# A recurrent attention block with a gated feed-forward block on one core: fewer, wider idle products, level one in one piece, and a shift behind a masked copy

## The chip, the core and the metric

The kernel runs on one core of a Trainium2 chip. The time is what the device takes for one execution, in microseconds (us). The engines have short names: PE (TensorE, the matrix array; its weight loads are shown apart as PEld), DVE (VectorE), ACT (ScalarE), POOL (GpSimd) and SP (SyncE, which here only issues transfers). Each engine runs its own instructions in order and waits for others through semaphores.

## What is computed

The first block is a linear attention with a decaying state, for 4 batches, 8 heads, 768 steps and head size 48. The second multiplies the result (3072 tokens of 384) by a weight to 2048, applies a gate, and multiplies back to 384. All is in float32.

```python
for t in range(S):
    cur = np.einsum('bhd,bhe->bhde', u[None] * kt, vt)
    y[:, :, t] = np.einsum('bhd,bhde->bhe', rt, state + cur)
    state = wt[:, :, :, None] * state + np.einsum('bhd,bhe->bhde', kt, vt)
x = y.transpose(0, 2, 1, 3).reshape(B * S, H * D)
h = x @ w_in
sp = np.maximum(h, 0.0) + np.log1p(np.exp(-np.abs(h)))
out = (h * erf(sp)) @ w_out
```

## The kernel before

The 768 steps are cut into 12 stages of 64. Stage s does the attention of its 64 steps for all batches and heads, while pieces of the feed-forward block of earlier stages run between its parts: six products against `w_in` are one piece of `hidden` (three contraction blocks for each of two blocks of features), and `project` multiplies by `w_out`.

**Levels.** Inside a stage the attention is built by doubling. At level L, `level_products` multiplies the keys of the left halves of blocks of 2^L steps by the queries of the right halves into a bank of PSUM called `pp` (there are two, used in turn). `take_level` then copies the masked part into `own` (a predicated copy on DVE), and `scale` multiplies keys and queries in place by the decays of their half blocks (on DVE, by totals that POOL makes), which the products of the next level need. At level one the products use `rk1`, where u is already multiplied in, and one DVE product with the mask `first` starts `own`. Six levels make a stage's 64 steps. Then `from_own` multiplies `own` by v into `y`, `fence` copies a few elements of y into `seen` so that others can wait for it, and `through_state` adds the carried state's part and lays y out as `xT`, which the feed-forward block reads. In stage 0 the last step of this is `hop`: three products with the 0/1 matrix `apart` shift rows, and DVE adds the result to xT.

**Stage 0** is `attend_first`. It has no older pieces to run beside it. So it has idle products, whose results nobody reads: `stay_warm(24)` at the beginning of the program, `stay_warm(4)` behind each half of level one's products, and `keep_busy(..., 4)` behind the products of levels two to five. Both multiply 128 columns at a time, `stay_warm` with the identity on both sides, `keep_busy` with a state that is still zero. The products go in two halves (batches of two), and so do the scalings of stage 0. The stages overlap at their borders: of the 32 products of stage 1's level one, twelve are issued behind level six of stage 0, twelve behind `through_state`, and the last eight in stage 1 itself, behind the first piece of `hidden`.

**Conversion of the weights.** The weights come as float64, two words an element, and are turned into float32 in 16 chunks (8 of `w_in`, 8 of `w_out`), each in stages with one letter: "l" the load (SP), "b" ACT scales the high word into a base in PSUM, "r" ACT scales the low word, "h" a shift on DVE, "o" an add on POOL, "j" the shift and the add. `send` runs the next chunk of each letter, `stages["h"](3)` a given chunk. The loads have three buffers, and a small copy on POOL or ACT into a buffer (`behind`) holds a load back until some other work is done.

**Order.** The kernel is written under a manual schedule: every engine runs its instructions in the order in which the Python code emits them. `place(n)` is called once a level by `attend`; it emits conversions (`convert_at`), feed-forward pieces (`beside`) and activations (`advance`). SP's queue has the loads in the same order of emission.

Lines for the prediction: L970 `stay_warm`, L976 `keep_busy`, L657 `level_products`, L880 and L1023 the product of level one with `first`, L667 the masked copy, L327 and L334 `scale`, L919 ACT's copies of level six in stage 0, L698 `fence`, L1131 the products of `hidden`, L1140 their copy out of PSUM, L258 and L260 "b", L275 "h", L288 "o", L768 the products for the state, L1162 `project`.

Of the kernel before, what the change touches and what calls it, by code (L numbers as in the profile page):

```python
# [11 lines left out]
FP32 = mybir.dt.float32  # L12
# [5 lines left out]
P = 128  # L18
# [4 lines left out]
NJ = 2  # L23
FG = 8
FT = 2

# [33 lines left out]
def kernel(  # L62
# [789 lines left out]
    def attend_first(xT):  # L852
# [10 lines left out]
        pp = products([P, NE, JP, HC])  # L863
        for half in halves:
            level_products(pp, by_pair(made), 1, half)
            stay_warm(4)
        nc.scalar.copy(first[:], mask_sb[:, 0, :])
        totals(1, part=slice(0, batch))
        for j in range(NJ):
# [15 lines left out]
        for level in range(2, LOG):  # L885
            pp = turns.pop("pp", None) or products([P, NE, JP, HC])
            for j, half in enumerate(halves):
                level_products(pp, first_pair, level, half)
                scale(0, level, batch=j)
            turns["pp"] = products([P, NE, JP, HC])  # L890
            keep_busy(turns["pp"], 4)
            take_level(own, pp, level)
            wait_for(1 << level - 1)
            if level == 2:
                totals(2, part=slice(batch // 2, batch))
            else:
                totals(*behind[level])
            if level == 2:
                stages["b"](0, 0)
                stages["b"](0, 1)  # L900
                stages["r"](0)
                for _ in prepare(1):
                    pass
                nc.sync.dma_start(out=vt[:], in_=v[0])
                stages["l"](1, own[:, 0, 2:3])
                nc.sync.dma_start(out=ws[1][:], in_=rkw[1][:, 2])
# [29 lines left out]
        stages["h"](1)  # L936
        totals(1)
        through_state(0, xT)
        level_products(turns["pp"], second, 1, range(3, 6))
        turns.pop("hop")()  # L940
        stages["r"](1)
        stages["o"](1)
# [23 lines left out]
    def stay_warm(times):  # L966

        for _ in range(times):
            ps = ps_m.tile([P, P], FP32, name="m")
            nc.tensor.matmul(ps[:], lhsT=ident[:], rhs=ident[:], start=True, stop=True)  # L970

    def keep_busy(pp, times):

        zeros = states[0][:].rearrange("p h n d -> p (h n d)")
        for _ in range(times):
            nc.tensor.matmul(  # L976
                pp[:].rearrange("p e n t -> p (e n t)")[:, :P], lhsT=ident[:],
                rhs=zeros[:, :P], start=True, stop=True, skip_group_check=True,
            )

    def attend(s, xT, early, place, behind):

        in_t, vt, made, _, _ = parts_of(s)
        K = in_t[:, 1]
        RK = by_pair(in_t)


        following = prepare(s + 1) if s + 1 < n_steps else iter(())
        own = made if s >= DIRECT else att.tile([P, NH, HC], FP32, name="own")

        if s == DIRECT:
            next(following)
        for level in range(near_log(s) + 1 if s == DIRECT else 1, LOG + 1):
            rk = by_pair(made) if level == 1 else RK
            pp = turns.pop("pp", None) or products([P, NE, JP, HC])
            if s == level == 1:
                send("br")
            elif s != 2 or level != 2:
                level_products(pp, rk, level)
            if level == LOG and s == DIRECT:  # L1000
                spread_blocks(s + 1, pp)
            if s == 1 and 2 < level:
                stages["h"](level + 1)
            scale(s, level)
            if s == 1 and level in turns["pending"]:
                turns["pending"].pop(level)()
            if s == 1 and level == 2:
                stages["h"](level + 1)
            if s == 1 and level > 1:
                nc.gpsimd.tensor_copy(out=block_sb[:, 0:1], in_=K[:, 0, 0:1])  # L1010
                for i in {2: (2, 3)}.get(level, (level + 1,)):
                    stages["o"](i)
            if s == 2 and level > 1:
                hold(K[:, 0, 0:1])
                send("o")
            if s != 1:
                early(level - 1)
            got = pp[:].rearrange("p e n t -> p (e n) t")
            if s == level == 1:
                place(0)  # L1020
                level_products(pp, rk, 1, range(6, JP))
            if level == 1:
                nc.vector.tensor_mul(  # L1023
                    own[:], got, first[:, None, :].to_broadcast([P, NH, HC])
                )
                if s == 1:
                    stages["h"](2)
            else:
                take_level(own, pp, level)
            if (s, level) == (DIRECT - 1, 4):  # L1030
                hold(K[:, 0, 0:1])
                fade_state(s)
            if level > 1 and (s, level) != (1, 4):
                next(following, None)
            if s == 2 and level == 1:

                def ahead():
                    turns["pp"] = products([P, NE, JP, HC])
                    level_products(turns["pp"], RK, 2)

                turns["ahead"] = ahead
            if (s, level) != (1, 1):
                place(level - 1)
            if (s, level) == (1, 4):
                next(following, None)
            if s == 1 and level in (3, 4):
                nc.sync.dma_start(out=loaded[2][0][:, level - 3], in_=rkw[2][:, level - 3])

        from_own(s, own, 1)
        ps = products([P, JP, P])  # L1050
        for n in range(JP):
            nc.tensor.transpose(ps[:, n, :], K[:, n, :], ident[:])  # L1052
        kT = att.tile([P, NH, D], FP32, name="kT", bufs=1)
        nc.scalar.copy(
            kT[:].rearrange("p (e n) d -> p e n d", e=NE),
            ps[:].rearrange("p n (e d) -> p e n d", e=NE)[..., :D],
        )
        if s != DIRECT - 1:
            fade_state(s)
        next(following, None)  # L1060
        place(LOG)
        if s == DIRECT - 1:
            for _ in range(3):
                mixing.send(nc.vector)

        ps = products([P, NC, JP, HC])
        state_part(s, kT, ps)
        from_own(s, own, 0)
        next_state(s, ps)
        for _ in following:  # L1070
            pass
        place(LOG + 1)
        through_state(s, xT)
        behind()
# [442 lines left out]
    with tc.manual_schedule(  # L1517
        engines={getattr(mybir.EngineType, x) for x in ("PE", "DVE", "Activation", "Pool", "SP")}
    ):
        stay_warm(24)  # L1520
        for t in states:
            nc.gpsimd.memset(t[:], 0.0)
        nc.gpsimd.memset(over_blocks[:], 1.0)
# [9 lines left out]
        for s in range(n_steps):  # L1533
# [7 lines left out]
            def place(n):  # L1541
# [7 lines left out]
                if s in ALONE:  # L1549
                    if s == 2 and not n:  # L1550

                        next(hids[0])
                        turns.pop("ahead")()
                    if (s, n) != (1, 0):
                        convert_at(n)
                    if (s, n) == (1, LOG - 1):
                        load_w(3)
# [4 lines left out]
                        nc.sync.dma_start(out=u_row[:], in_=u_rows)  # L1562
                    if s == 2 and not n:
                        beside(s, next(places))
                        advance(STAGES[s][n])
                        return
                    advance(STAGES[s][n])
# [131 lines left out]
```

## Time and profile before

| | |
|---|---|
| median of 3 runs | 587.57 us (587.5 to 589.57) |
| profiled execution, its own time | 589.73 us |
| its span, first to last instruction | 587.9 us |
| busy: PE, DVE, ACT, POOL | 577.2, 427.4, 355.0, 242.2 us |
| mean granted clock of TensorE | 0.991 |
| PE busy from 0 to 32.5 / 32.5 to 71 / 71 to 587.9 | 28.65 / 35.20 / 513.38 us |

The page of the profile gives the busy time of each engine, and the span in 40 equal slices with the granted clock of TensorE in tenths. The trace can also be asked for windows (busy time of each engine in a stretch, with the granted clock, the share of the DMA engines and the rate), for a timeline (start, duration, engine, line, operation, written tile <- read tiles, shape, count, and in brackets the idle time before it and what ended it) and for waits. A matrix product in float32 appears as two records on PE and two weight loads on PEld. Matmuls are pipelined and their ends are modelled, so the start of the next group tells more than the end of the last. A releaser named "issue" means that the profile shows nothing that the engine waited for.

### The profile page before, as it was taken

How to read it: one execution, taken by the hardware profiler on the slowest of the kernel's cores; microseconds unless marked ns; L12 is line 12 of the kernel's file. 1: busy time of each engine (PE TensorE's matmuls, PEld its weight loads, DVE VectorE, ACT ScalarE, POOL GpSimd, SP SyncE). 2: the span in 40 equal slices, each digit the busy share in tenths (PEclk: the TensorE clock that was granted, in tenths of full speed). 3: DMA queues.
4: the chain of work that ended last, by engine and by line, in shares of the span. 5: the costliest groups of instructions: out<-in, count | busy, mean ns of one | idle time of the engine just before them, and what ended most of it. 6: DMA issues, size and time to landing. Idle time of an engine off the chain costs nothing.

```text
span 587.9 us, 16633 instructions
## 1 busy us (share of the span) xinstructions
PE 577.2 (98%) x7302; PEld 501.3 (85%) x7302; DVE 427.4 (73%) x451; ACT 355.0 (60%) x478; POOL 242.2 (41%) x263
## 2 busy tenths in 40 slices
PE   8989899999999999999999999999999999999997
PEld 8877788668768857899899899899899899988997
DVE  5677495799796699699599599599599537256530
ACT  3376698817544398675775765765865861387700
POOL 2187266520884776277077077067065000000000
PEclk9699999999999999999999999999999999999999
DMA  7388173532226226236236236235231101000111
GB/s 256 107 288 341 56 276 108 222 81 83 97 75 190 42 95 197 46 108 198 49 106 199 47 107 198 46 108 163 47 107 28 19 10 35 1 2 1 28 28 27
DMA packets 52057, 62.04 MB, mean 106 GB/s; under 512 B 33392, under 2 KB 38800, under 8 KB 50960
## 3 DMA queue, kind: packets, MB, share of 16 engines
q1 hardware_dynamic: 51360, 60.58, 33.8%
q8 instruction: 57, 0.93, 0.7%
q10 hardware_dynamic: 624, 0.39, 0.3%
q14 instruction: 16, 0.13, 0.1%
HBM read 51.60 MB, written 8.27 MB: 102 GB/s over the span
## 4 chain that ended last, share of the span: by engine, by line
PE 87%; ACTq 0%; ACT 0%; issue 0%; DVE 0%
PE m L1131 32%; PE m L1244 28%; PE m L1162 11%; PE pp L1332 4%; PE pp L657 4%; PE y L1332 2%; PE y L689 2%; PE y L712 2%; PE pp L768 1%; PE pp L1052 1%; PE pp L1244 0%; ACTq L756 0%; PE pp L781 0%; ACT y L260 0%; DVE o L1276 0%
## 5 line engine op out<-in xcount | busy, mean ns | idle before, releaser
L1131 PE MATMUL m<-xT,w_in_sb 128*128 128x256 f32 x960 | 214.2, 381 | 1.5 <-ACT y L260 1.5
L1131 PEld LDWEIGHTS m<-xT,w_in_sb 128*128 128x128 f32 x960 | 180.1, 190 | 26.5 <-ACT y L260 1.6
L334 DVE TENSOR_TENSOR in<-in,tot_sb 128x1024 f32<-128x1024 f32 (+1 forms) x55 | 77.7, 1412 | 20.7 <-PE pp L657 19.7
L1140 ACT COPY h<-m 128x512 f32<-128x512 f32 x80 | 46.4, 580 | 61.7 <-PE m L1131 61.7
L1162 PE MATMUL m<-w_out_sb,h 128*128 128x384 f32 x192 | 64.3, 491 | 0.0
L1162 PEld LDWEIGHTS m<-w_out_sb,h 128*128 128x128 f32 x192 | 35.7, 190 | 23.5
L1244 PE MATMUL m<-mixed,h 128*128 128x192 f32 x256 | 45.6, 331 | 0.0
L1244 PE MATMUL m<-w_out_sb,h 128*128 128x192 f32 x256 | 44.8, 329 | 0.0
L1244 PEld LDWEIGHTS m<-mixed,h 128*128 128x128 f32 x256 | 41.4, 190 | 0.9
L1091 ACT ACT_TABLE_LOAD x30 | 38.5, 1283 | 6.0 <-DVE h L1096 5.6
L1244 PEld LDWEIGHTS m<-w_out_sb,h 128*128 128x128 f32 x256 | 41.6, 190 | 0.3
L657 PEld LDWEIGHTS pp<-in 48*48 48x48 f32 (+4 forms) x2368 | 31.9, 125 | 11.4 <-issue 6.5
L1244 PE MATMUL m<-w_out_sb,room 128*128 128x192 f32 x240 | 41.5, 326 | 0.0
L464 POOL TENSOR_TENSOR words<-words,own 128x384 f32<-128x384 f32 x21 | 31.0, 1476 | 22.5 <-DVE words L495 12.8
L457 POOL TENSOR_TENSOR own<-rest 128x384 f32<-128x384 f32 x7 | 10.4, 1482 | 71.3 <-ACT o L1250 44.4
L505 POOL TENSOR_TENSOR words<-words 128x384 f32<-128x384 f32 x28 | 39.7, 1447 | 0.0
L1087 ACT ACT_TABLE_LOAD x30 | 38.5, 1283 | 1.8 <-issue 1.3
L1244 PEld LDWEIGHTS m<-w_out_sb,room 128*128 128x128 f32 x240 | 39.4, 190 | 0.0
L657 PE MATMUL pp<-in 48*48 48x32 f32 (+4 forms) x2368 | 35.9, 211 | 1.8 <-issue 1.8
L617 POOL COPY faded<-s 128x1 f32<-128x1 f32 x10 | 12.4, 1240 | 53.8 <-DVE s L623 53.8
L530 DVE TENSOR_REDUCE sums<-rk 128x16 f32<-128x768 f32 (+2 forms) x31 | 31.6, 1021 | 0.0
L505 POOL TENSOR_TENSOR rk<-words 128x384 f32<-128x384 f32 x28 | 31.4, 1154 | 0.0
(200 smaller groups left out, 998.9 us busy)
## 6 DMA issues: line engine op xcount, KB each, us to landing
in<-in_rkw SPq DMA_DIRECT2D x8, 1024.0 KB, 5.4
words<-in_moe_w_in SPq DMA_DIRECT2D x16, 384.0 KB, 6.5
words<-in_moe_w_out SPq DMA_DIRECT2D x16, 384.0 KB, 6.1
words<-in_rk_rows SPq DMA_DIRECT2D x8, 768.0 KB, 7.3
w<-in_rkw SPq DMA_DIRECT2D x11, 512.0 KB, 6.4
v<-in_v SPq DMA_DIRECT2D x12, 384.0 KB, 5.7
out<-o SPq DMA_DIRECT2D x45, 96.0 KB, 2.8
in<-in_rkw SPq DMA_DIRECT2D x7, 512.0 KB, 5.3
```

The lines of the kernel that those rows point to most:

```text
L334: nc.vector.tensor_mul(halves, halves, view(tots[level - 1], 0, [[1, n], [2, nb], [0, half]]))
L464: engine.tensor_mul(to, to, of[:, :, None, :].to_broadcast([P, NEAR // 2 // half, half, D]))
L505: engine.tensor_mul(to[:, i], r[:, half:], k[:, part * rows + i, None].to_broadcast([P, half, D]),)
L530: nc.vector.tensor_reduce(out=to, in_=of, axis=mybir.AxisListType.X, op=ALU.add)
L657: nc.tensor.matmul(to, lhsT=rk(1, n)[rows(e), s0 : s0 + m], rhs=right, start=True, stop=True,)
L1087: nc.scalar.activation(sp_room, chunks[0], AF.Softplus)
L1091: nc.scalar.activation(at, sp_room, AF.Erf)
L1131: nc.tensor.matmul(ps[:, ff, :], lhsT=w_in_sb[:, g * FG + f + ff, kk * P : (kk + 1) * P], rhs=xT[:, kk, :], start=kk == 0, stop=kk == KT - 1,)
L1140: nc.scalar.copy(h[:, f : f + FT, :], ps[:])
L1162: nc.tensor.matmul(ps[j][:], lhsT=gs[g][:, f, j * C : (j + 1) * C], rhs=w_out_sb[:, g * FG + f, :], start=g + f == 0, stop=g == NG - 1 and ...
L1244: nc.tensor.matmul(to, lhsT=a[:, f], rhs=b[:, f], start=start and f == 0, stop=f == FG - 1, skip_group_check=True,)
L1332: nc.tensor.matmul(to[:, e], lhsT=a[:, 2 * i + e], rhs=b, start=start and not k, stop=True, skip_group_check=True,)
```

## The change

- The 24 opening idle products become 36 small ones (64 x 64 x 64, in the two opposite quarters of the array in turn) and 5 wide ones of 256 columns. Behind each half of level one, 4 of 128 columns become 2 of 256. Behind levels two to five, 4 of 128 become one of 384.
- The last eight products of stage 1's level one are issued with the twelve before them, ahead of the hop's shift products and so ahead of the first piece of `hidden`. DVE's product L1023 keeps its place among DVE's instructions.
- In stage 1, level two, the shift and the add of chunk 3 are emitted behind the masked copy, not before it.
- In stage 2, the conversion at its first place is emitted behind the piece `beside`; ACT's copy of that piece so comes ahead of the conversion's two ACT operations.

By the order in which the built programs stand, SP and POOL run the same instructions in the same order as before. On DVE one shift changes places with one masked copy, and L1023 loses its wait for PE. On ACT one copy changes places with two activations. On PE the idle products differ, and 8 products (16 records) move up.

```diff
+FEW = 36
@@ attend_first
             level_products(pp, by_pair(made), 1, half)
-            stay_warm(4)
+            stay_warm(2)
@@
             turns["pp"] = products([P, NE, JP, HC])
-            keep_busy(turns["pp"], 4)
+            keep_busy(turns["pp"])
             take_level(own, pp, level)
@@
         through_state(0, xT)
-        level_products(turns["pp"], second, 1, range(3, 6))
+        level_products(turns["pp"], second, 1, range(3, JP))
         turns.pop("hop")()
@@
     def stay_warm(times):
 
         for _ in range(times):
-            ps = ps_m.tile([P, P], FP32, name="m")
-            nc.tensor.matmul(ps[:], lhsT=ident[:], rhs=ident[:], start=True, stop=True)
-
-    def keep_busy(pp, times):
+            ps = ps_m.tile([P, NC, P], FP32, name="m")
+            nc.tensor.matmul(
+                ps[:], lhsT=ident[:], rhs=ident[:, None, :].to_broadcast([P, NC, P]),
+                start=True, stop=True,
+            )
+
+    def keep_busy(pp):
 
         zeros = states[0][:].rearrange("p h n d -> p (h n d)")
-        for _ in range(times):
-            nc.tensor.matmul(
-                pp[:].rearrange("p e n t -> p (e n t)")[:, :P], lhsT=ident[:],
-                rhs=zeros[:, :P], start=True, stop=True, skip_group_check=True,
-            )
+        nc.tensor.matmul(
+            pp[:].rearrange("p e n t -> p (e n t)")[:, :DM], lhsT=ident[:],
+            rhs=zeros[:, :DM], start=True, stop=True, skip_group_check=True,
+        )
@@ attend
-            if s == 1 and level == 2:
-                stages["h"](level + 1)
             if s == 1 and level > 1:
                 nc.gpsimd.tensor_copy(out=block_sb[:, 0:1], in_=K[:, 0, 0:1])
-                for i in {2: (2, 3)}.get(level, (level + 1,)):
-                    stages["o"](i)
+                stages["o"](2 if level == 2 else level + 1)
@@
-            if s == level == 1:
-                place(0)
-                level_products(pp, rk, 1, range(6, JP))
             if level == 1:
                 nc.vector.tensor_mul(
                     own[:], got, first[:, None, :].to_broadcast([P, NH, HC])
@@
             else:
                 take_level(own, pp, level)
+                if s == 1 and level == 2:
+                    stages["h"](3)
+                    stages["o"](3)
@@
-            if (s, level) != (1, 1):
-                place(level - 1)
+            place(level - 1)
@@ the program's start
-        stay_warm(24)
+        few = ps_m.tile([P, NC, P], FP32, name="m")
+        for n in range(FEW):
+            here = rows(n & 1, HC)
+            nc.tensor.matmul(
+                few[here, 0, :HC], lhsT=ident[here, here], rhs=ident[here, here],
+                start=True, stop=True,
+            )
+        stay_warm(5)
@@ place
-                    if (s, n) != (1, 0):
+                    if n:
                         convert_at(n)
@@
                     if s == 2 and not n:
                         beside(s, next(places))
+                        convert_at(n)
                         advance(STAGES[s][n])
                         return
```

## The prediction

> **What bounds the kernel now.** I read the clock row of the page first, then the windows, then the timeline of PE and of DVE. Times are microseconds (us) from the start of the span. A product in float32 shows as two records, so "x48" is 24 products.
>
> ```profile
> PE 577.2 (98%) x7302; PEld 501.3 (85%) x7302; DVE 427.4 (73%) x451; ACT 355.0 (60%) x478; POOL 242.2 (41%) x263
> PEclk9699999999999999999999999999999999999999
> ```
>
> TensorE (PE) is busy for 98% of the span, and the granted clock is low in the second of forty slices only. These windows cut the span where the clock changes:
>
> ```profile
> 2.06:5.47 3.41, 3.41 (x16) 3.41 (x17) 2.82 (x6) 0.59 (x3) 0.65 (x2) 1.00 0.91 293
> 5.47:8.88 3.41, 3.41 (x27) 3.41 (x26) 2.72 (x11) 1.11 (x5) 1.09 (x2) 1.00 0.71 228
> 15.71:19.12 3.41, 2.06 (x71) 1.91 (x71) 2.23 (x3) 3.05 (x9) 0.71 (x3) 0.98 0.23 48
> 19.12:22.50 3.38, 3.38 (x73) 3.09 (x72) 2.52 (x5) 0.00 (x0) 0.68 (x4) 0.50 0.87 339
> 25.85:29.25 3.40, 3.40 (x115) 3.08 (x118) 1.36 (x3) 1.20 (x4) 0.25 (x2) 0.50 0.02 5
> 39.49:42.90 3.41, 2.50 (x87) 1.96 (x89) 2.46 (x3) 3.13 (x4) 3.04 (x2) 1.00 1.00 394
> 71.00:587.90 516.90, 513.38 (x5872) 445.62 (x5872) 384.15 (x392) 316.28 (x404) 207.97 (x210) 1.00 0.31 91
> ```
>
> The columns are PE, PEld, DVE, ACT, POOL, clock, DMA share, GB/s. The clock is 0.50 from 19.12 to 29.25, after a stretch in which PE was busy for 2.06 of 3.41; a stretch with 2.50 (39.49) kept it at 1.00. At the start the column says 1.00, but the same idle products give 16 records, then 27: the array is slow until about 5.3. After 71 PE idles 3.5 in 517. So an instant saved before PE is full stays saved, if what PE needs later starts earlier too. The front:
>
> ```profile
> 2.00 8.01 PE L970 MATMUL m<-ident 128*128 128x128 f32 x48 [2.00 <-POOL ident masks.py:199]
> 9.94 0.69 PE L657 MATMUL pp<-rk 48*64 48x64 f32 x32
> 13.56 1.11 PE L657 MATMUL pp<-in 48*62 48x32 f32 x64
> 17.57 0.84 PE L657 MATMUL pp<-in 48*60 48x32 f32 x42 [1.35 <-issue]
> 19.74 1.72 PE L657 MATMUL pp<-in 48*56 48x32 f32 x64
> 21.39 2.07 PE L976 MATMUL pp<-s,ident 128*128 128x128 f32 x8
> 23.40 1.51 PE L657 MATMUL pp<-in 48*48 48x32 f32 x64
> 24.83 2.07 PE L976 MATMUL pp<-s,ident 128*128 128x128 f32 x8
> 12.58 1.22 DVE L880 TENSOR_TENSOR own<-pp,first 128x1024 f32<-128x1024 f32 x1 [3.06 <-PE pp L657]
> ```
>
> PE looks full, but with products whose result nobody reads, and they are in the way. The operands of the first half of level one are ready at 6.43 (ACT's last copy into rk), of the second at 7.64 (DVE's), and PE reaches them at 9.94 and 11.75. DVE idles 3.06 for it. At half clock a level takes PE 3.5 (19.74 to 23.40, 23.40 to 26.84), of which 2.0 are four idle products. Stage one, later:
>
> ```profile
> 35.82 1.23 DVE L1023 TENSOR_TENSOR own<-pp,first 128x1024 f32<-128x1024 f32 x1 [1.43 <-PE pp L657]
> 40.44 0.96 DVE L275 TENSOR_SCALAR w_in_sb<-y 128x768 int32<-128x768 int32 x1 [1.39 <-ACT y L258]
> 42.71 0.94 PE L768 MATMUL pp<-v,kT 64*48 64x48 f32 x64 [0.91 <-DVE own L667]
> ```
>
> DVE waits for PE's level one; then a shift waits 1.39 for ACT with the masked copy behind it, and PE waits 0.91 for that copy.
>
> **The change part by part**
>
> Prices per record. 256 wide, full clock: 0.227 (12 of L1131 from 32.56 to 35.29); 384 wide: 0.335 (L1162, 16 in 5.36). Half clock: twice that, an estimate. 64 wide in alternate quarters: 0.019 at full clock (32 from 9.94 to 10.56), 0.029 to 0.038 at half (24 from 27.85, next group at 28.54, own end 28.77).
>
> 1. *Opening idle products* (48 records become 72 small and 10 wide). Small at the slow rate: 72 x 0.034 = 2.4, from 2.00 to 4.4. Two wide to 5.3 at 0.455, eight at 0.227: level one starts at 7.1 instead of 9.94. The rows bound the opening: it took 3.3 of work at the start, 10.1 later. I take 5.3, because PE is as full as in the first stretch; at the other end (12.1) DVE's first product comes 3.2 later than below.
>
> 2. *Between the halves* (8 narrow records become 4 wide, twice). 7.1, products 0.62, idle 0.91, second half from 8.65 to 9.3, idle 0.91: level two starts at 10.2 instead of 13.56. DVE's two scalings (7.81, 1.71 long) hold it until 9.52, so its product L880 starts at 9.55 instead of 12.58. The gain on the chain is 3.0, not 3.4; what is late next is DVE.
>
> 3. *Idle products of levels two to five* (8 narrow records become 2 of 384): 0.67 at full clock, 1.34 at half, instead of 1.1 to 1.5 and 2.0. DVE: 9.55 + L880 1.22, scale 1.29, masked copy 1.32 = 13.4 for level three's scale (18.06 before). PE by then: level two from 10.2 to 11.3, idle to 11.95, level three to 13.0. The 1.35 stall named "issue" may come back here; up to 0.4 of it is hidden behind the masked copy, and all but 0.25 where it falls in the first half. Then, at full clock, PE needs 1.05 + 0.67 a level and DVE 1.29 + 0.70 + 0.1 = 2.1, so DVE sets it. POOL's marker copy and totals (0.07 + 0.18 + 0.40 after a scale) fit beside the 0.70. Scales: 13.4, 15.5, 17.6 (before 18.06, 20.84, 24.39); last masked copy ends at 19.65. Level six lies beside it. ACT's four copies (L919) start at 19.7 instead of 27.98; its own preparations before that ended at 18.76 and wait for a load, not for PE. The fence, which starts 1.71 after those copies, is at 21.4 instead of 29.69: **8.3 gained**.
>
>    Does the clock hold? Between 12.3 and 15.7 PE has 0.7 of level three, 0.67 idle product and 1.05 of level four, and a piece of the next: some 2.5 of 3.4. That is at the row that held (2.50) and above the one that fell (2.06). I take "holds". If it falls at 15.7, PE sets two levels at 1.5 + 1.34 = 2.85, and the fence comes at about 22.8; half clock until 25.9 at worst would slow the hop and the first piece by up to 2 more. Price: 1.4 to 3.4.
>
>    The Trainium skill ("TensorE: Matmul & The Clock Gate", Part 1, "What's actually happening") says the clock falls after an idle window of about 3.4 us and is full again after one busy window of that length. The row disagrees on both: it fell after a gap of 1.35 and took 10.1 of busy PE to return. By the page the changed front keeps its clock for certain, and the forecast would be the one that I reach with "holds"; by the row the fall stays possible and costs 1.4 to 3.4. The same section says that the window runs free and does not start with the kernel, which speaks against a fixed opening at 5.3; no single trace can show that.
>
> 4. *All of level one ahead of the first piece.* 16 records move before the three shift products. From the rows 0.3 to 0.5, partly in a gap of 0.1 to 0.3 where PE waits for ACT's y3: +0.1 on the first piece, which POOL's add of its weights (ends 32.28, piece at 32.50) holds up anyway. Behind them on PE wait the hop, then DVE's xT adds. DVE's L1023 no longer waits (1.43); the shift behind it waits for ACT's y (ends 35.87) and gains 1.0. PE's transposes start some 0.7 earlier.
>
> 5. *Shift of chunk three behind the masked copy.* The copy fills the 1.39; the shift cannot start before ACT's y (40.40), so it isn't later. POOL's add of chunk three stays where it is in POOL's order; its weights are used at 47.31, 4 after it ends. The 0.91 on L768 goes. But the next scale (43.35) stands behind the shift of chunk four, and level five's behind that of chunk five, whose data ACT waited 3.2 for (46.84). So of 1.6 that PE gains by L768 most is given back at level five. Ends 0 and 1.6; I take 0.3 for steps 4 and 5, near the lower end, because the load sets the later row.
>
> 6. *Stage two: a piece's eviction ahead of a conversion on ACT.* The copy at 74.47 moves before L260 at 72.86, which starts about 1.5 later, and so does the erf behind it (75.07); PE has pieces of its own until 76.4. Taken as 0; if DVE's shift at 75.01 (on which level three's products wait) comes 0.3 later, it costs 0.3. SP's and POOL's orders are unchanged.
>
> Sum: 8.3 + 0.3 = 8.6. The profiled execution took 589.73 (span 587.9 and 1.8 around it): 581.1. It lies 2.2 above the median 587.57; where these lie the trace can't tell. If around the front, the median gains 6.4 (581.1), if not, 8.6 (579.0). Between them: **580.0**.
>
> **The rivals**
>
> - *The clock falls all the same.* For: 2.5 of 3.4 is close to the row that fell. Against: less waiting. 580.0 + 1.4 to 3.4 = 581.4 to 583.4.
> - *The clock opens late.* For: the same array needed 10.1 once. Against: the first row's 3.3. 580.0 + up to 3.2 = 583.2.
> - *The front's gain isn't carried.* For: from 32.66 to 46.30 the DMA engines are busy 0.97 to 1.00, and ACT waits 5.6 there for weights. Against: these loads are issued behind the fence and the hop, and the DMA engines are nearly still from 23 to 31.5, so they move with them; what the front itself needs (1.3 MB from 13.5, behind 0.6 MB still under way) ends by 19 at some 350 GB/s. If half is lost: 584.3; if nearly all, "same".
> - *Slower: the small and the zero-fed products do not open the clock at all until the pieces run.* For: zero-fed products filled 19.12 to 25.85 and it stayed at 0.50. Against: it opened after 25.85 to 29.25, filled mostly by products of 32 and 64 columns. Then level one starts at 9.0, each level takes 2.85, the fence is at 29.1, and hop and first pieces (2.7 more for each 12 records) run slow: +2 to +5, 590 to 593. It decides if the half clock lasts beyond about 27.
>
> **How the numbers follow.** A measurement tells about 0.5% (2.9) from no change. Clock holds: 0.50 (own range 577.5 to 582). Falls: 0.23. Opens late, with or without a fall: 0.12. Not carried: 0.09, half of it within 0.5%. Never opens early: 0.06. The range is from 577.0 (579.0, with 1.6 instead of 0.3 from steps 4 and 5, rounded up) to 585.5 (583.2, with a fall of 1.4, and 0.9 of lost carrying). Faster 0.85, within 0.5% 0.09, slower 0.06.
>
> **What the profile after would show.** Level one's products at about 7, DVE's first own product at 9.5 without a wait; clock 1.00 between 9 and 30; masked copies 2.1 apart; the fence near 21.4 and the first piece near 24; no wait of L768 for the masked copy; the rest of the span as long as before. I am wrong if the clock row shows half speed beyond 26, if level one still starts after 9, or if PE's idle time between the first piece and stage two grows by what the front gained.

## The result and the profile after

The changed kernel takes 585.76 us (median of 17 runs, 583.91 to 588.13) against 588.27 for the kernel before (17 runs beside it): 0.9949 of it, with a 95% interval from 0.9932 to 0.9966. That is 3.0 us by the ratio (2.5 between the medians), where the forecast was 580.0, 7.6 below the earlier median of 587.57, and the range ended at 585.5. The profiled execution took 584.51, its span 582.7.

The page of the changed kernel, the rows that answer to those of before:

```profile
PE 572.3 (98%) x7304; PEld 493.7 (85%) x7304; DVE 426.8 (73%) x451; ACT 355.0 (61%) x478; POOL 242.1 (42%) x263
...
PEclk9799999999999999999999999999999999999999
```

The second slice still loses clock, if less. Windows of the changed kernel, cut where the clock changes (PE, PEld, DVE, ACT, POOL, clock, DMA share, GB/s):

```profile
16.20:19.61 3.41, 2.30 (x124) 1.65 (x117) 2.52 (x4) 2.16 (x6) 1.20 (x5) 1.00 0.87 252
19.61:23.03 3.42, 1.81 (x86) 1.11 (x75) 2.83 (x5) 0.00 (x0) 0.35 (x2) 1.00 0.38 138
23.03:26.45 3.42, 2.61 (x73) 2.36 (x77) 0.67 (x2) 2.48 (x6) 0.43 (x1) 0.50 0.02 5
26.45:29.86 3.41, 3.41 (x74) 3.02 (x67) 1.39 (x4) 2.21 (x7) 3.19 (x4) 0.50 0.64 201
71.00:582.70 511.70, 507.97 (x5848) 440.99 (x5847) 378.86 (x387) 312.42 (x399) 205.92 (x208) 1.00 0.31 90
```

The clock fell at 23.03 and came back at 29.86: half speed beyond 26, one of the three signs by which the prediction said it would be wrong. From 71 on PE idles 3.7, as before (3.5): what was won ahead of 71 is kept. Where it was won, and where not, is in the timeline of the changed kernel (all engines; line numbers are one or so higher than before, L1522 are the small products):

```profile
2.00 4.10 PE L1522 MATMUL m<-ident 64*64 64x64 f32 x72 [2.00 <-POOL ident masks.py:199]
...
8.38 0.69 PE L658 MATMUL pp<-rk 48*64 48x64 f32 x32
...
10.90 1.23 DVE L881 TENSOR_TENSOR own<-pp,first 128x1024 f32<-128x1024 f32 x1 [1.47 <-PE pp L658]
...
18.10 0.91 PE L979 MATMUL pp<-s,ident 128*128 128x384 f32 x2 [1.11 <-DVE in L328]
...
19.63 1.30 DVE L328 TENSOR_TENSOR in<-in,tot_sb 128x512 f32<-128x512 f32 x2 [0.91 <-POOL tot_sb L357]
...
20.64 0.79 PE L658 MATMUL pp<-in 48*32 48x32 f32 x60
...
23.47 0.32 PE L658 MATMUL pp<-in 48*32 48x32 f32 x4 [2.05 <-issue]
...
23.84 1.52 ACT L920 COPY own<-pp 32x256 f32<-32x256 f32 x4 [5.48 <-PE pp L658]
...
25.78 0.17 DVE L699 COPY seen<-y 128x16 f32<-128x16 f32 x1 [3.33 <-PE y L690]
...
30.40 2.75 PE L1130 MATMUL m<-xT,w_in_sb 128*128 128x256 f32 x12
```

The fence and the first piece in the profile before:

```profile
29.69 0.17 DVE L698 COPY seen<-y 128x16 f32<-128x16 f32 x1 [2.48 <-PE y L689]
...
32.56 2.80 PE L1131 MATMUL m<-xT,w_in_sb 128*128 128x256 f32 x12
```

Level one starts at 8.38 (before 9.94, forecast 7.1), DVE's first own product at 10.90 (12.58, forecast 9.55), the fence comes at 25.78 (29.69, forecast 21.4), the first piece at 30.40 (32.56). PE has two gaps that the forecast did not have. One of 1.11 stands before the idle product of level four; the other, of 2.05, lies inside level six, after 60 of its 64 records, and its releaser is "issue": nothing that the profile shows was waited for.

The count of records tells what these gaps are. Up to the gap in level six PE has run 72 + 10 + 32 + 4 + 32 + 4 records, then five times 64 and four times 2, less 4: 478. The gap at 18.10 stands behind 350. In the kernel before, the gap of 1.35 inside level three stands behind 48 + 32 + 8 + 32 + 8 + 64 + 8 + 22 = 222. All three lie on one grid of 128 records, which are 256 instructions with their weight loads. And a queue that carries instructions, q8, moves one block of 16 KB shortly ahead of each gap's end: at 15.0 before (the gap ends at 17.57), at 15.5 and 21.0 after (the gaps end at 18.10 and 23.47). Times of blocks here and below are the starts of windows of 0.25 in which they are seen, so they can be up to 0.25 early. In the whole span q8 moves 57 blocks, and the 7304 records of PE make 57.1 times 128. The row of the DMA queues of the changed kernel from 21.00 to 21.25 (instructions, packets, MB, share of 16 engines):

```profile
q8 instruction: 1, 0.02, 23.8%
```

So the theory for the experiments, called A: PE gets its instructions in blocks of 128 records, a block comes some 2.5 us after its transfer, and where the front runs 128 records faster than blocks come, PE stands still. The rival, B: the shortfall is the half clock. The label of the gap at 18.10 ("DVE in L328") would speak for a plain wait; its place on the grid and the block 2.6 earlier speak against it, and so does a later run (the late load below), in which the same idle product starts at 17.37 while that scaling, begun at 17.18, still runs.

### The profile page after: what moved, and what is told of

It reads as the page before. It is cut to its first block, busy times and chain, and to the rows that moved or that the text cites. A ratio compares the mean times of both kernels' runs of the same rounds, so it can differ in the third digit from the quotient of the medians.

```text
span 582.7 us, 16637 instructions
## 1 busy us (share of the span) xinstructions
PE 572.3 (98%) x7304; PEld 493.7 (85%) x7304; DVE 426.8 (73%) x451; ACT 355.0 (61%) x478; POOL 242.1 (42%) x263
## 4 chain that ended last, share of the span: by engine, by line
PE 86%; DMA 2%; DVE 0%; ACT 0%; issue 0%; SPq 0%; ACTq 0%
PE m L1130 31%; PE m L1243 28%; PE m L1161 11%; PE pp L1331 4%; PE pp L658 3%; PE y L1331 2%; PE y L690 2%; PE y L713 2%; PE pp L769 1%; DMA words<-in_moe_w_out 1%; PE pp L1051 1%; PE pp L1243 0%; DMA xT<-y 0%; PE pp L782 0%; DVE y L276 0%; DVE w_out_sb L281 0%
## 5 line engine op out<-in xcount | busy, mean ns | idle before, releaser
L1090 ACT ACT_TABLE_LOAD x30 | 38.5, 1283 | 5.9 <-DVE h L1095 5.4
L658 PEld LDWEIGHTS pp<-in 48*48 48x48 f32 (+4 forms) x2368 | 30.3, 120 | 13.5 <-issue 6.8
L1086 ACT ACT_TABLE_LOAD x30 | 38.5, 1283 | 2.3 <-issue 1.8
L658 PE MATMUL pp<-in 48*48 48x32 f32 (+4 forms) x2368 | 34.1, 206 | 2.1 <-issue 2.1
```

The source lines that it names most:

```text
L658: nc.tensor.matmul(to, lhsT=rk(1, n)[rows(e), s0 : s0 + m], rhs=right, start=True, stop=True,)
L1086: nc.scalar.activation(sp_room, chunks[0], AF.Softplus)
L1090: nc.scalar.activation(at, sp_room, AF.Erf)
```

## The experiments

Ratios are to the kernel before, timed beside each run, with 95% intervals. Fence and first piece are from the profiles, each of one execution. How many stretches of half clock (3.4 each) the other executions had is counted from their mean granted clock, which one stretch lowers by 0.003; where in the span they lie is not known.

**One part alone.** The idle products alone on the kernel before:

```diff
-        stay_warm(24)
+        (36 small products)
+        stay_warm(5)
...
-            stay_warm(4)
+            stay_warm(2)
-            keep_busy(turns["pp"], 4)
+            keep_busy(turns["pp"])
```

> The kernel before with the new idle products alone (level one still in three parts, shift of chunk 3 still ahead of the masked copy). Theory A (instruction supply): PE's front runs out of instructions, which come in blocks of 128 records, so the front gains only 2 to 4 us at the fence (25.8 there in the changed kernel, 29.7 before) and the rest of the change's gain belongs to the other parts. Expected here 0.2 to 0.45% faster than before, a gap of PE of over 1 us named issue after the 478th record (level six), and stage one as long as before (38.6 from the first piece to the two pieces at its end). Theory B (clock): the shortfall against the forecast is the half clock; then the runs without half clock are 6 us or more faster than before.

Measured: 0.9945 [0.9921, 0.9970]; 585.59 as median of 10. The fence is at 25.02, a gap of 1.23 lies after the 60th record of level six, and stage one lasts 38.7 from the first piece (29.73) to the two pieces at its end (68.44). So the idle products bring all that the change brings. One of its executions had no half clock and took 583.21; the kernel before without half clock takes 587.8 (mean of five): 4.6 us, not the 6 or more of theory B. The one execution of the changed kernel without half clock took 584.19, 3.6 less.

The rest alone, the changed kernel with the old idle products:

```diff
-        (36 small products)
-        stay_warm(5)
+        stay_warm(24)
...
-            stay_warm(2)
+            stay_warm(4)
-            keep_busy(turns["pp"])
+            keep_busy(turns["pp"], 4)
```

> The changed kernel with the old idle products (24, 4 and 4 of 128 columns): only level one in one piece, the shift behind the masked copy and the reordered conversion. Forecast of record for these parts: 0.3 us. Reading of the trace after: 3.4 us from the first piece to the two pieces at the end of stage one (35.2 there, 38.6 before). If that reading holds, 0.4 to 0.6% faster than before and this part carries most of the change; if these gains came from the shorter front, 0 to 0.15%.

Measured: 1.0006 [0.9980, 1.0031]. The timeline of PE in this kernel shows why:

```profile
41.71 0.91 PE L768 MATMUL pp<-v,kT 64*48 64x48 f32 x64
42.55 2.86 PE L1127 MATMUL m<-xT,w_in_sb 128*128 128x256 f32 x12
46.30 1.03 PE L657 MATMUL pp<-in 48*56 48x32 f32 x64 [0.89 <-DVE s L625]
...
52.49 0.30 PE L657 MATMUL pp<-in 48*48 48x32 f32 x4 [1.54 <-issue]
```

L768 no longer waits, as forecast, and the next level's products wait 0.89 for DVE in its place; DVE is late because it waits twice 0.97 there for ACT's base of a weight chunk (its shifts at 41.36 and 43.29); ACT in turn waited 1.34 for DVE's masked copy and 0.21 for DVE's shift, by the profile. The 3.4 by which stage one is shorter in the profile after (35.1 instead of 38.5) is therefore no work of these parts by themselves.

**Fewer records ahead of level one.**

```diff
-        few = ps_m.tile([P, NC, P], FP32, name="m")
-        for n in range(FEW):
-            (a small product)
-        stay_warm(5)
+        stay_warm(8)
```

> The changed kernel with 8 wide opening products instead of 36 small and 5 wide (16 records instead of 82), so 66 records fewer ahead of level one, which starts at 7 to 8.5 as before. Theory A: instructions arrive in blocks, the block borders stay at records 222, 350 and 478 of PE, so the gaps move: two records into level four, between level five and its idle product, and in the first or second y group; no gap at the end of level six, fence 1 to 2.5 earlier than 25.8, 0.2 to 0.4% faster than the changed kernel. Theory B or a wait for DVE: the gaps of 1.1 and 2.1 stay where they are (idle product of level four, end of level six) and the time too.

Measured: 0.9910 [0.9877, 0.9943], 583.39 as median of 5. Its timeline of PE around the places where the gaps were:

```profile
17.23 0.95 PE L658 MATMUL pp<-in 48*48 48x32 f32 x64
18.26 0.91 PE L979 MATMUL pp<-s,ident 128*128 128x384 f32 x2
19.10 0.91 PE L658 MATMUL pp<-in 48*32 48x32 f32 x64
20.27 0.58 PE L658 MATMUL pp<-rk 48*64 48x64 f32 x24 [0.26 <-DVE own L668]
20.64 1.03 PE L690 MATMUL y<-own,v 64*48 64x64 f32 x32
22.03 0.32 PE L690 MATMUL y<-own,v 64*48 64x64 f32 x4 [0.37 <-DVE seen L699]
22.62 0.59 PE L690 MATMUL y<-own,v 64*48 64x64 f32 x26 [0.27 <-issue]
```

Levels five and six run without a gap; the one left lies in the second y group, four or so records into it, 476 records from the start (the trace has the program's full count up to there), two short of the grid, and a block moved at 20.0. The fence is at 21.71, close to the forecast of 21.4, with DVE's level the bound: the sum of step 3 nearly held for a PE that has its instructions. That it is met within 0.3 is partly luck: DVE's first own product starts 0.8 later than forecast (10.37), and its levels take 1.9 each instead of 2.1. The clock stayed at 1.00 through the front. Of 8.0 gained at the fence against the profile before, 7.4 are there at the first piece (25.18) and 6.5 in the span; here DVE holds the next group up by 0.60 and two gaps named "issue" (1.14 and 0.76) come in stage one.

**More records in the same time.**

```diff
-FEW = 36
+FEW = 68
...
-            here = rows(n & 1, HC)
+            here, there = rows(n & 1, HC), rows(n >> 1 & 1, HC)
...
-                few[here, 0, :HC], lhsT=ident[here, here], rhs=ident[here, here],
+                few[n & 1][there, 0, :HC], lhsT=ident[here, there], rhs=ident[here, here],
```

> The changed kernel with 68 small opening products in four quarters of the array instead of 36 in two: nearly the same array time (136 records at 0.028, end near 6 as in the changed kernel) but 64 records more. Theory A (instructions come in blocks of 128 records): the borders fall a level earlier, gaps near the start of level two, at the start of level four and before the idle product of level five; the front is 1.5 to 3 us longer than in the changed kernel and the time 0.2 to 0.5% worse than that kernel, 0 to 0.3% better than before. Without a limit of supply: same time as the changed kernel, gaps where they were.

Measured: 0.9955 [0.9927, 0.9982], and the small products end at 5.93. The timeline of PE:

```profile
16.73 1.03 PE L658 MATMUL pp<-in 48*56 48x32 f32 x64 [0.79 <-DVE own L668]
17.69 0.91 PE L979 MATMUL pp<-s,ident 128*128 128x384 f32 x2
18.53 0.92 PE L658 MATMUL pp<-in 48*48 48x32 f32 x62
22.11 0.27 PE L658 MATMUL pp<-in 48*48 48x32 f32 x2 [2.67 <-issue]
```

Level five starts behind 416 records now, so the gap behind its 62nd is at 478: the grid again, a level earlier, and 2.67 long. The gap of 0.79 at 16.73, at level four's start, stands behind 350, with a block at 14.25. The time is not told apart from the changed kernel's (0.9949): the expected loss of 0.2 to 0.5% is not shown. The fence, at 26.47, is 0.7 later, less than the 1.5 to 3 expected.

**The price of a small product.** The same spread over four quarters, with 36 as in the change:

```diff
-            here = rows(n & 1, HC)
+            here, there = rows(n & 1, HC), rows(n >> 1 & 1, HC)
...
-                few[here, 0, :HC], lhsT=ident[here, here], rhs=ident[here, here],
+                few[n & 1][there, 0, :HC], lhsT=ident[here, there], rhs=ident[here, here],
```

> The changed kernel with its 36 small opening products spread over all four quarters of the array instead of two opposite ones, the count unchanged. If the price of 0.056 us a record (forecast 0.034) comes from two quarters sharing the array's time, 0.027 to 0.035 now: they end at 4.0 to 4.6 instead of 6.03 and level one starts up to 1 us earlier. If it is an issue price of the slow clock, still 6.0. Theory A says that little of this reaches the fence (under 0.5 us), since the blocks of instructions don't come sooner; without a limit of supply all of it would (0.15% faster than the changed kernel).

The timelines of this kernel and of the changed one differ in the price:

```profile
2.00 2.20 PE L1522 MATMUL m<-ident 64*64 64x64 f32 x72 [2.00 <-POOL ident masks.py:199]
4.27 3.91 PE L971 MATMUL m<-ident 128*128 128x256 f32 x10
```

72 records take 2.27, 0.032 each, against 4.03 and 0.056. So the price depends on how many quarters the products turn over: my row (24 from 27.85) was of products that turn over four, the new ones over two. Level one starts only 0.3 earlier (8.10), because in this execution the wide products ran slow until about 7.4. 0.9915 [0.9883, 0.9948]: better than the changed kernel by more than expected, though the intervals overlap. The fence, at 24.80, is 1.0 earlier, where theory A said under 0.5: the block behind 478 moved at 20.0 instead of 21.0, and PE, at half clock from 17.5 to 24.4, reached that record too late to wait for it.

**Why a block is late.** The changed kernel, with 1.3 MB of weights and decays issued behind level five, not behind level two:

```diff
                 nc.sync.dma_start(out=vt[:], in_=v[0])
-                stages["l"](1, own[:, 0, 2:3])
+            if level == 5:
+                stages["l"](1, own[:, 0, 16:17])
                 nc.sync.dma_start(out=ws[1][:], in_=rkw[1][:, 2])
```

> The changed kernel with the loads of weight chunk 1 and of the second stage's decays (1.3 MB, issued from 15.7 in the changed kernel) held back until after the masked copy of level five. Theory A1 (a block of instructions is late because it shares the DMA engines with this data): the blocks after the second border land sooner, the gaps at the idle product of level four (1.1) and at the end of level six (2.1) shrink to under half, the fence comes 1 to 2 us earlier than 25.8; the weights then come later, so the time is 0 to 0.2% better than the changed kernel. Theory A2 (a block takes its 4.5 to 5.5 us whatever the load): gaps unchanged, time the same or up to 0.3% worse.

Measured: 0.9944 [0.9925, 0.9963]. The timeline of PE:

```profile
17.37 0.91 PE L980 MATMUL pp<-s,ident 128*128 128x384 f32 x2
...
21.09 0.25 PE L658 MATMUL pp<-in 48*32 48x32 f32 x4 [0.19 <-issue]
...
25.35 0.34 PE L658 MATMUL pp<-rk 48*64 48x64 f32 x6 [0.94 <-issue]
28.00 2.07 PE L732 MATMUL m<-y,mixed 128*128 128x256 f32 x4 [2.31 <-ACT y L721]
```

The gap of 1.11 is gone and that of 2.05 is 0.19, at the same record. The block for it moved at 18.5 instead of 21.0, though PE had started the block before it only 0.7 earlier (17.37 for 18.10). The fence is at 22.90. So this block was late because data moved, and for it A1 stands. For the gap of 1.11 the run shows nothing of the kind: its block had moved at 15.5 in the changed kernel, just when the issue of the 1.3 MB began (15.66), too early to be held up by them, and comes at 15.0 here, in both as the transfers issued earlier run out. The gain is lost at once: ACT, which must copy y for the hop, stands behind a conversion whose weights now come late, and PE waits 2.31.

**The clock.**

```diff
-            rhs=zeros[:, :DM], start=True, stop=True, skip_group_check=True,
+            rhs=ident[:, None, :].to_broadcast([P, KT, P]), start=True, stop=True,
+            skip_group_check=True,
```

> The changed kernel with its four idle products of 384 columns fed with the identity instead of zeros, same count and shape. If products fed with zeros don't count for the clock, the half clock gets rarer: 13 of 17 executions of the changed kernel had two stretches of 3.4 us at half clock; here under half of the executions, and the median 0.1 to 0.3% better. If the clock falls because PE idles while it lacks instructions, no difference: most executions with two stretches, same median within 0.15%.

Measured: 0.9932 [0.9904, 0.9960], 585.48 as median; all five executions had two stretches at half clock, as most of the changed kernel's, and the gap in level six is 2.33. What the idle products are fed with makes no difference that these runs can tell.

**Towards a better kernel.** The wide opening, cut:

```diff
-        stay_warm(8)
+        stay_warm(6)
...
-            stay_warm(2)
+            stay_warm(1)
```

> The kernel with 8 wide opening products, cut to 6, and one wide product instead of two behind each half of level one: level one from 6.9 to 7.4, level two from 9.3 to 10 instead of 11.2. DVE's first own product then starts at 9.5, held by its own scalings, 0.7 earlier. Theory A: 8 records fewer, borders a little later in the work, the gain of 0.7 kept at the fence in part: 0.05 to 0.15% better than with 8 wide ones (0.9895 to 0.9905 of before). If the opening then is too thin for the clock, the first opening of it slips a stretch of 3.4 us and the time is 0.1 to 0.3% worse.

Measured: 0.9867 [0.9836, 0.9898], 582.57: clearly better than the changed kernel, and more than forecast, though not told apart from the wide opening. The profile does not show where more than there was won: level one starts at 7.27 and level two at 9.78, but the fence comes at 21.93 (21.71 with the wide opening) and the first piece at 27.16 (25.18). A gap of 1.09 stands in level six after the 350th record.

Without the idle products of levels two to five:

```diff
-            keep_busy(turns["pp"])
```

> The kernel with the short wide opening, without the four idle products behind levels two to five (8 records fewer). DVE's scaling and masked copy set a level there (1.8 to 2.4), so the idle products (0.85) are worth nothing on the chain: time the same within 0.1%, or 0.05 to 0.1% better by the records saved. If they hold the clock, it falls in nearly all executions, two or more stretches of 3.4 us, and the time is 0.2 to 0.5% worse than 0.9867 of before.

Measured: 0.9864 [0.9825, 0.9902], 581.60 as median of 4. The clock falls as the second half of the expectation said, four stretches in all four executions; the price that it named for that did not come, and the time is the same, as the first half said. Its timeline of PE:

```profile
11.16 1.60 PE L658 MATMUL pp<-in 48*60 48x32 f32 x64 [1.01 <-DVE in L328]
13.52 1.72 PE L658 MATMUL pp<-in 48*56 48x32 f32 x64 [0.77 <-DVE in L328]
15.43 1.51 PE L658 MATMUL pp<-in 48*48 48x32 f32 x64 [0.19 <-DVE in L328]
17.34 1.30 PE L658 MATMUL pp<-in 48*32 48x32 f32 x64 [0.40 <-DVE in L328]
18.70 0.92 PE L658 MATMUL pp<-rk 48*64 48x64 f32 x24
```

At half clock 64 records take 1.3 to 1.7, and PE still waits for DVE before levels three to six: slow products cost nothing there, and no instruction is late there. The fence is at 20.65, the earliest but one.

Two other places for the load of 1.3 MB, in the kernel with the short wide opening; ahead of level two:

```diff
         totals(2, part=slice(0, batch // 2))
+        stages["l"](1, t5[:, 1, 0, NP - 1, 1:2])
+        nc.sync.dma_start(out=ws[1][:], in_=rkw[1][:, 2])
...
-                stages["l"](1, own[:, 0, 2:3])
-                nc.sync.dma_start(out=ws[1][:], in_=rkw[1][:, 2])
```

> The kernel with the short wide opening, with the loads of weight chunk 1 and of the second stage's decays (1.3 MB) issued ahead of level two, at about 10.5, right behind the second stage's keys, not behind the masked copy of level two. Theory A1 (blocks of instructions are late while this data moves): the data is through by 18, the block fetched at 20.25 there comes at 18 to 19.5, the gap in level six (1.09) falls under 0.4 and the fence comes up to 1 us earlier than its 22.0: 0.1 to 0.25% better than the short wide opening (0.9843 to 0.9857 of before). If instead the blocks fetched around 11.5 and 16 get later by it, a gap of 0.5 to 1.5 appears in levels three or four and the time is the same or 0.2% worse.

Measured: 0.9906 [0.9872, 0.9940]. I was wrong: the gap in level six grew to 2.21. The block that ends it is the one that moved at 16.25 in the kernel with the short opening, not the one at 20.25, and with the data ahead of it, it moved at 18.0. The fence is at 23.27. Behind level four:

```diff
-                stages["l"](1, own[:, 0, 2:3])
+            if level == 4:
+                stages["l"](1, own[:, 0, 8:9])
                 nc.sync.dma_start(out=ws[1][:], in_=rkw[1][:, 2])
```

> The kernel with the short wide opening, with the same 1.3 MB issued behind the masked copy of level four (about 17) instead of level two (14). Theory A1: the block fetched at 16.25 comes a little sooner, the one at 20.25 shares the engines with the data and comes no sooner, so the gap in level six stays (0.8 to 2); the weights land at about 22 to 23, in time for the fence. Time within 0.1% of the short wide opening or up to 0.2% worse. If the place of this load didn't matter: the same time, the same gap of 1.09.

Measured: 0.9882 [0.9847, 0.9916]. Again the gap in level six went otherwise than I wrote: it is gone, the block moved at 15.0, and the fence is at 20.60. All four executions had at most one stretch at half clock. The weights were late, though, not in time as I wrote: PE waits 1.52 for ACT's y, and the time is not better. Both misses have one cause, the block that I had taken for the wrong one; with the right one, the three places of the load in this kernel agree with A1.

**One grid in all profiles.** The thirteen profiles together tell what the gaps are. Up to 76 us their timelines of PE print 27 gaps that end with "issue". Counted from the start of the program, they stand behind 222 records (2 gaps), 350 (2), 476 or 478 (8), 604 (2), 731 (1), 858 or 859 (3) and 985 or 986 (9), and nowhere else: steps of 126 to 128, in kernels that reach these records in different levels and at different times, in stage one too (the gap of 1.54 above stands behind 986). In five kernels, the changed one among them, the gap behind 350 is put down to DVE. Each gap up to 26 ends 2.2 to 3.1 after a block has moved.

## Why the prediction was wrong, point by point

**The bound of the front (step 3) failed.** Its sum has no term for the supply of instructions, only the sentence that the stall named "issue" of 1.35 "may come back here", with "all but 0.25" of it hidden. It is not one stall but a limit: a block for every 128 records, each some 2.5 behind its transfer, and the transfer later the more data moves. At the forecast's 2.1 a level PE wants 128 records every 4.1; in the profile after the blocks moved at 10.5, 15.5 and 21.0. Of the 4.4 by which the fence is later than forecast, 1.35 were there at DVE's first own product (10.90 for 9.55). Almost all the rest are the two gaps: 1.11 at the idle product of level four, of which DVE's next scale feels 0.7 (19.63, 2.0 late), and 2.05 in level six, after which ACT's copies are 4.1 late (23.84 for 19.7). Where the records ahead are fewer, the fence comes at 21.71, close to the sum.

How early a block can come is read from the rows, not tested by a run of its own. Where few data move, the next block moves 0.9 to 1.2 after the end of a gap in the levels (seven profiles; after the change 24.5 behind 23.47), where data move 1.6 to 3.3 after it (21.0 behind 18.10). With some 2.5 from there to the first record, 128 records take about 3.5 at best, an estimate from these rows. So the forecast's 4.1 was in reach, with little other data on the way.

The Trainium skill, "Runtime: NRT & Kernel Launch", section "Instruction fetch mechanics", states the same block, 16 KiB or 256 instructions, and that crossing from one to the next is mostly hidden. The block agrees with the grid; the cost does not: 1.11 and 2.05 here, 2.67 with more records.

**The opening (step 1)** was mis-sized: 0.056 a small record, not 0.034, because its row was of products over four quarters; the four-quarter run gives 0.032. Level one was 1.3 late from it, and PE, not DVE, was late next in step 2 (DVE waited 1.47).

**The clock.** "Holds", at 0.50, was the wrong choice: 13 of 17 executions of the changed kernel had two stretches at half clock (mean 586.0), four had one or none (584.3). The difference, 1.7, lies in the rival's 1.4 to 3.4, though these executions may differ in more than the clock; in the profile it shows in the way from the fence to the first piece, 4.6 instead of 2.9. The clock fell behind the row 19.61: PE busy for 1.81 of 3.42, with the gap of 2.05 in it. Where that gap is absent and the idle products remain, 8 of 9 executions had at most one stretch in two kernels (wide opening, load behind level four), but none of four with four quarters and two of six with the late load. So the gap goes with the fall in part and is not shown to be its only cause. Nor does PE's busy time decide it, by which the prediction had judged (2.06 fell, 2.50 held):

```profile
14.13:17.54 3.41, 2.29 (x91) 1.52 (x84) 3.41 (x6) 3.31 (x10) 1.06 (x4) 1.00 0.60 179
17.54:20.96 3.42, 3.42 (x67) 2.19 (x68) 1.95 (x4) 0.00 (x0) 0.67 (x3) 0.50 0.80 315
...
21.49:24.90 3.41, 1.87 (x63) 1.66 (x63) 1.02 (x2) 2.21 (x6) 1.70 (x2) 1.00 1.00 339
24.90:28.31 3.41, 3.41 (x16) 2.53 (x14) 3.33 (x4) 1.65 (x4) 3.29 (x3) 1.00 0.90 310
```

The first two windows are of the four-quarter run, where the clock fell after 2.29 of 3.41; the last two of the load behind level four, where it held after 1.87. What decides it is left open.

The Trainium skill ("TensorE: Matmul & The Clock Gate", Part 1) says that the clock is set by a window of about 3.4 us that runs free, and falls after an idle one. The measured stretches agree with the window, 10.2, 6.8 and 3.4 long, and the first opening moved between executions (5.4 in the profile before, 6.0 after, 7.7 with the idle products alone). That a fall needs a whole idle window is not what the rows show: it came after windows with PE busy 1.81 and 2.29.

**The kernel it was measured against.** The profiled execution of before, 2.2 above its median, was one with three stretches at half clock. Of 42 executions of that kernel whose clock is known, 22 had at most one (mean 588.2), five had three (590.6). The difference, 2.4, is the size of the 2.2, and in the profile the three stretches lie in the front. So the 2.2 probably lay there, the first of my two ways, and of the 8.6 counted on that trace 2.2 was this execution's, not the kernel's; I had taken half. It rests on five executions and is not shown for this one.

**Steps 4 and 5** were taken as 0.3 and measured as nothing (1.0006); the interval reaches 1.2 below and 1.8 above that, so 0.3 is neither shown nor excluded. What L768 gains is given back as the forecast said, at a scale behind the shifts, but at level four, where it had put most at level five, and the shifts wait for ACT's base, not for a load. **Step 6** cost nothing that can be seen in the same run. That stage one is 3.4 shorter in the one pair of profiles is not explained by these parts alone: in other profiles it lasts 35 to 39, and it was longest both where the first piece came early (38.7 with the wide opening) and with the idle products alone (38.7). The supply of instructions has a part in it: with the wide opening two gaps on the grid (1.14 and 0.76) lie in it, in the profile after none. What else sets it in one execution is left open.

**Carried to the end** it was: after 71 PE idles 3.7 against 3.5.

The sum for the pair of profiles: 8.6, less 4.4 at the fence, less 1.8 on the way to the first piece, plus 3.1 in stage one, is 5.5; the spans differ by 5.2, and the 0.3 left are lost behind stage one. Between medians it is 2.5, and 3.0 by the ratio, because the trace before was of a long execution (1.5 above 588.27) and that after of a short one (1.25 below 585.76).

## What to carry to other kernels

A stretch of many small products can be bound by the supply of instructions: count them from the start of the program, see whether gaps named "issue" fall on one grid, and look in the DMA rows for the block that ends each. Filler that keeps an engine busy should then be few and wide (0.9867 here, against 0.9949). Data that moves while a block is due delays the block, but holding the load back did not pay here: the fence came earlier twice, and each time PE then waited for ACT, whose weights were late. And before a sum is made on one trace, look whether that execution is a usual one: here the clocks of other executions, known only later, said that it was not.

## What the hardware showed that I had not expected

- PE's instructions came in blocks of 16 KB, 128 product records; gaps ended 2.2 to 3.1 us after a block's transfer was seen, and with 1.3 MB of data moving at the time a block came 2.5 later (21.0 against 18.5), 0.7 of it because PE was later at the block before.
- Small products of 64 x 64 x 64 at the slow clock took 0.056 a record over two quarters of the array and 0.032 over four.
- Idle products fed with zeros and with the identity were not told apart in the clock: two stretches of half clock in five of five executions, as in 13 of 17.
- Without the idle products behind the levels the clock was at half for four stretches in every execution, and the kernel was still the fastest by its median, 581.60 (0.9864), beside the one with them (582.57, 0.9867).
- The clock fell after a window with PE busy 2.29 of 3.41 in one profile and held after one with 1.87 in another.
